# Attention and a routed expert layer on one core: three shifts in the order of the expert stage

## The chip, the cores and the metric

One Trainium2 chip, one of its cores. The metric is the device time of one execution in microseconds (us). Engine names as in the profile: PE is TensorE (PEld its weight loads), DVE is VectorE, ACT is ScalarE, POOL is GpSimd, SP is the queue that issues most DMAs.

## The reference

Block-causal attention, then a layer of eight experts in which every expert takes exactly `cap` tokens. Cut to what matters:

```python
# attention: q, k, v are (8, 8, 576, 64); causal in blocks of 64
attn = softmax(where(block_i >= block_j, q @ k.T / 8, -1e9))
x = (attn @ v).transpose(0, 2, 1, 3).reshape(4608, 512)
# experts: E = 8, cap = 4608 // 8 = 576, w1 (8, 512, 1024), w2 (8, 1024, 512)
logits = x @ w_gate
for idx in argsort(-logits.flatten()):          # the best pairs (token, expert) first
    tok, e = idx // E, idx % E
    if assigned[tok] < 0 and counts[e] < cap:
        assigned[tok] = e; counts[e] += 1
for e in range(E):
    m = assigned == e
    out[m] = maximum(x[m] @ w1[e], 0) @ w2[e]
```

## The kernel before

Two stages run one after the other: attention, up to about 343 us, and the experts. Each matrix of the expert layer is kept as a sum of two float16 parts, so a product takes three matmuls.

**Who sets the order.** The kernel's engines take their instructions in the order in which the program emits them. That order is made by a small planner (`Sched`) while the program is built. Each strand of work is a Python generator; a `yield` names an engine, an estimated cost in ns, and events that must have been set. The planner picks the strand that can start first by its own clock (`sc.now`); a lower number of priority goes ahead, and a strand of a later number may fill in where it ends early enough. `sc.set(e)` sets an event at the planned time, and `sc.ev[e]=t` sets it at a time written by hand. Such a time shapes only the written order: on the chip an instruction waits for its data, and all behind it on its engine wait with it.

**Routing.** Experts are filled one at a time, in an order that the data decide. `route(k)` searches the threshold that gives some expert `cap` tokens: 14 steps, each with counts on VectorE (L810) and ScalarE (L752), a product on TensorE (`tot`, L824) and a comparison (L827). From the result come the expert's number, with which `weights(k)` starts its loads, a prefix product (`po`, L879 to L886) that gives each token its place, and `invert`, which turns places into a list of tokens: one-hots `OH`, `OL`, `RH` on VectorE (L920, L924, L926, L927), 36 small products (`pe`, L935), a second product (`ps`, L942), and the index tile `ix` (L945). The generator `out()` (L905 to L907) takes the tokens of this expert out of the logits `Lm` and then starts `route(k+1)`, whose first instruction is L721. `route(k)` also waits until the expert `k-2` is at its middle (`mid`). The last routing has no search, since one expert is left; `hold` keeps back its two products.

**Tokens.** `gather(k)` issues five indirect DMAs on POOL (L1007), 128 rows each and 64 in the last, into `xg`. For the first two experts `flip` transposes them on TensorE (L1017), eight transposes to a block, and ScalarE and VectorE copy the halves into `X` (L1021, L1022); for the others a DMA on SP transposes them (L1032).

**Weights.** Eight pieces for each expert, loaded over SP (L993). ScalarE scales and rounds them (L972, L976), POOL subtracts to get the second part (L978); for the first four pieces of the first two experts it is L965 on ScalarE and L967 on VectorE.

**The expert.** `ffn(k)`: `h` (L1057) in two parts of the tokens, 256 and 320 wide, then `y` (L1082, and L1086 for the last 64 tokens). ScalarE and VectorE take `h` out of PSUM (L1043, L1045); ScalarE takes `y` (L1065), and POOL scatters it to the output (L1073).

Of the kernel before, what the change touches and what calls it, by code (L numbers as in the profile page):

```python
# [614 lines left out]
class Moe:  # L615
# [96 lines left out]
    def route(s,k):  # L712
# [155 lines left out]
        def full():  # L868
            V.tensor_tensor(s.es,s.es,ei,op=OP.subtract)
            V.tensor_scalar(u,oh,-8.0,None,op0=OP.mult)  # L870
            V.tensor_tensor(Lm,Lm,be(u),op=OP.add)
            sc.busy(D,520)
# [27 lines left out]
        if not last:  # L900

            def out():
                yield D,600
                if k==0: full()
                V.tensor_tensor(q[:,2],q[:,2],MM[:,0],op=OP.add)  # L905
                V.tensor_scalar(q[:,3],q[:,2],8.0,None,op0=OP.mult)
                V.tensor_tensor(Lm,Lm,b3(q[:,3]),op=OP.subtract)  # L907
                sc.set(('Lm',k+1))
                sc.add(s.route(k+1),0,sc.now)
            if k>1: sc.add(out(),0,sc.now)  # L910
            else: s.late=out
        yield from s.invert(k,L16,h2)
    def hold(s,k):

        s.sc.ev['hold',k]=s.sc.now+(8000 if k==s.E-1 else 0)
    def invert(s,k,L16,h2):
        nc=s.nc; rp=s.rp; C=s.C; V=nc.vector; sc=s.sc
        yield D,440
        OH=rp.tile([P,20,C],F16,tag="OH",name=f"OH{k}"); RH=rp.tile([P,2,20,C],F16,tag="RH",name=f"RH{k}")
        V.tensor_tensor(OH,s.io5,h2[:,None,:].to_broadcast([P,20,C]),op=OP.is_equal)  # L920
        if k<2: nc.scalar.activation(RH[:,1],OH,AF.Copy,scale=s.pc)
        yield D,700
        OL=rp.tile([P,32,C],F16,tag="OL",name=f"OL{k}",bufs=1)
        V.tensor_tensor(OL,s.iom,L16[:,None,:].to_broadcast([P,32,C]),op=OP.is_equal)  # L924
        yield D,440 if k<2 else 800
        V.tensor_tensor(RH[:,0],OH,s.tok,op=OP.mult)  # L926
        if k>1: V.tensor_scalar(RH[:,1],OH,s.pc,None,op0=OP.mult)  # L927
        else: sc.add(s.late(),0,sc.now)
        s.hold(k)
        yield T,350,'rt',('hold',k)  # L930
        tk=sc.take(); ps=s.ps.tile([P,512],F32,tag="rt",name=f"pe{k}")

        for c in range(C):
            g=32*(c%4)
            nc.tensor.matmul(ps[g:g+32,:40].rearrange("p (a b) -> p a b",a=2),lhsT=OL[:,:,c],rhs=RH[:,:,:,c],start=(c<4),stop=(c>=C-4))  # L935
        t=rp.tile([P,2,20],F16,tag="ixt",name=f"ixt{k}")
        yield D,100
        V.tensor_copy(t,ps[:,:40].rearrange("p (a b) -> p a b",a=2)); sc.set(tk)
        yield T,150,'rt'
        tk=sc.take(); ps=s.ps.tile([P,512],F32,tag="rt",name=f"ps{k}")  # L940
        for b in range(4):
            for a in range(2): nc.tensor.matmul(ps[32*b:32*b+32,0:5],lhsT=s.b32[:,a],rhs=t[:,a,b::4],start=(a==0),stop=(a==1))  # L942
        ix=rp.tile([P,5],I32,tag="ix",name=f"ix{k}",bufs=3)
        yield D,82
        V.tensor_copy(ix,ps[:,:5])  # L945
        sc.set(tk)
        sc.add(s.gather(k,ix),1,sc.now); sc.set(('ix',k))
        if k==0:

            s.wu=s.ps.tile([P,512],F32,tag="g",name="warm",bufs=4)  # L950
            for n in range(s.NWU): nc.tensor.matmul(s.wu,lhsT=s.ones,rhs=OL.rearrange("p a b -> p (a b)")[:,:512],start=True,stop=True)
            sc.free[T]=max(sc.free[T],sc.now)+213*s.NWU+1500
        s.ix[k]=ix
# [45 lines left out]
    def gather(s,k,ix):  # L999
        nc=s.nc; fp=s.fp; sc=s.sc  # L1000
        tl=[]
        for m in range(5):
            n=P if m<4 else 64
            yield G,1038,('ffn',k-2),('xm',k-1,m)
            if m==0: X=s.X[k]=fp.tile([P,8,576],F16,tag="X",name=f"X{k}")
            xg=fp.tile([P,1024],F16,tag="xg",name=f"xg{k}_{m}",bufs=5)
            nc.gpsimd.indirect_dma_start(out=xg[:n],out_offset=None,in_=s.xd,in_offset=bass.IndirectOffsetOnAxis(ap=ix[:n,m:m+1],axis=0))  # L1007
            sc.soft(728,('xg',k,m))
            sc.nolat()
            if m==4: sc.set(('gi',k))  # L1010
            sc.add(s.flip(k,m,n,xg,X),1,sc.now)
# [138 lines left out]
```

## Time and profile before

| | |
|---|---|
| median of 3 runs | 794.29 us (793.48 to 797.81) |
| profiled execution | 791.57 us |
| its span, first to last instruction | 789.8 us |
| granted TensorE clock, mean | 0.975 |
| busy share: PE, DVE, ACT, POOL | 91%, 72%, 68%, 59% |

A profile line such as `421.12 0.62 PE L1017 MATMUL xt<-m_idh,xg ... x8 [1.78 <-DMA xg<-x,ix]` gives the start, the duration, the engine, the source line, the tiles, how many instructions were merged, and, in brackets, how long the engine was idle before it and what ended that. In the list of waits the three numbers are us in total, times, and the longest. In the table of windows each engine has its busy us and, in brackets, its instructions; PEclk is the granted share of TensorE's clock. Ends of matmuls are modelled, so one that is followed at once can seem to last longer than the step from its start to the next start.

### The profile page before, as it was taken

What the parts mean: (1) busy time and instruction counts of PE and PEld (TensorE: products, weight loads), DVE (VectorE), ACT (ScalarE), POOL (GpSimd) and SP (SyncE); (2) the same over time, 40 slices, a digit from 0 to 9 for tenths busy, and PEclk for the clock granted to TensorE, in tenths of its full rate; (3) what the DMA queues carried; (4) which work ended last, traced back from release to release, by engine and by line L of the source; (5) the groups of instructions that cost most, each with busy time, mean ns of one, the idle gap of its engine ahead of it and who ended that gap; (6) DMA issues with size and microseconds to landing.
All of it is one profiled execution on the core that took longest, in us unless ns stands there. A gap on an engine that the chain in (4) does not pass through costs nothing.

```text
span 789.8 us, 19021 instructions
## 1 busy us (share of the span) xinstructions
PE 715.5 (91%) x6528; PEld 476.6 (60%) x6528; DVE 570.4 (72%) x2310; ACT 539.2 (68%) x1455; POOL 466.5 (59%) x509
## 2 busy tenths in 40 slices
PE   5779998899989999936998999999999999999995
PEld 3556776667767777724545747647466475574752
DVE  6899798998899889577988978769686793620210
ACT  5788888888988898715836868594975848283210
POOL 5788888898889876413413447373763907764001
PEclk9899999999999999966999999999999999999998
DMA  9879999999998993347026076481926639851001
GB/s 202 160 150 174 214 189 224 172 151 229 205 192 178 216 181 77 91 106 252 23 98 230 8 245 150 176 199 67 279 71 220 145 103 259 260 136 41 21 20 40
DMA packets 244305, 121.51 MB, mean 154 GB/s; under 512 B 200816, under 2 KB 227312, under 8 KB 244208
## 3 DMA queue, kind: packets, MB, share of 16 engines
q1 hardware_dynamic: 238320, 101.42, 56.7%
q0 software_dynamic: 5888, 18.88, 7.6%
q8 instruction: 51, 0.84, 0.4%
q14 instruction: 46, 0.38, 0.2%
HBM read 71.32 MB, written 18.87 MB: 114 GB/s over the span
## 4 chain that ended last, share of the span: by engine, by line
PE 42%; ACT 3%; DMA 3%; DVE 3%; issue 3%; POOL 1%; SPq 0%; POOLq 0%; another core or an unknown queue 0%; ACTq 0%; DVEq 0%
PE h L1057 23%; PE y L1082 15%; PE y L1086 2%; DMA raw<-in_moe_w_dram 1%; DMA out_dram<-yo,ix 1%; DMA xg<-x,ix 1%; POOL xg L1007 1%; ACT W L976 1%; ACT ja L752 1%; ACT raw L972 1%; DVE OL L924 1%; DVE h L897 1%; PE pe L935 1%; PE tot L824 1%; DVE jk L810 0%
## 5 line engine op out<-in xcount | busy, mean ns | idle before, releaser
L438 POOL TENSOR_TENSOR P<-P,m 128x320 f32<-128x320 f32 (+8 forms) x285 | 209.5, 770 | 49.6 <-DVE m L430 32.5
L1057 PE MATMUL h<-X,W 128*128 128x320 f16 (+3 forms) x1536 | 195.7, 286 | 0.6 <-issue 0.4
L1057 PEld LDWEIGHTS <-W 128*128 128x128 f16 x1536 | 142.0, 98 | 44.3 <-issue 4.7
L416 ACT ACTIVATE P<-psb,m 128x576 f32<-128x576 f32 (+8 forms) x288 | 149.5, 543 | 27.5 <-DVE m L409 18.7
L1082 PE MATMUL y<-W,HH 128*128 128x512 f16 x512 | 152.7, 380 | 0.0
L978 POOL TENSOR_TENSOR W<-raw,W 128x1024 f16<-128x1024 f32 x56 | 118.4, 2135 | 41.6 <-ACT W L976 36.0
L405 DVE TENSOR_REDUCE m<-psb 128x1 f32<-128x576 f32 (+8 forms) x288 | 124.8, 480 | 12.3 <-PE psb L380 11.8
L463 PE MATMUL psb<-mident,P 128*128 128x128 f32 x800 | 106.3, 281 | 13.2 <-POOL P L438 5.9
L1073 POOL DMA_INDIRECT out_dram<-yo,ix x40 | 39.3, 982 | 113.7 <-ACT yo L1065 77.5
L380 PEld LDWEIGHTS <-qT 128*64 128x64 f16 x1408 | 76.6, 111 | 43.6 <-issue 28.9
L463 PEld LDWEIGHTS psb<-mident,P 128*128 128x128 f32 x800 | 87.7, 142 | 24.5 <-POOL P L438 8.5
L380 PE MATMUL psb<-kT,qT 128*64 128x288 f16 (+8 forms) x704 | 89.6, 281 | 11.7 <-ACT P L416 10.9
L498 PE MATMUL psb<-PT,V 128*64 128x448 f32 (+5 forms) x776 | 97.2, 388 | 2.3 <-DVE PT L446 1.8
L1043 ACT ACTIVATE HH<-h 128x320 f16<-128x320 f32 (+3 forms) x128 | 52.3, 411 | 67.7 <-PE h L1057 63.3
L1082 PE MATMUL y<-W,HL 128*128 128x512 f16 x256 | 97.2, 380 | 0.0
L1007 POOL DMA_INDIRECT xg<-x,ix x40 | 40.9, 1023 | 83.0 <-DVE ix L945 38.9
L1045 DVE SCALAR_TENSOR_TENSOR HL<-h,HH 128x320 f16<-128x320 f32 (+3 forms) x128 | 56.9, 452 | 42.5 <-ACT HH L1043 39.4
L444 ACT ACTIVATE PT<-psb 128x512 f32<-128x512 f32 (+1 forms) x165 | 82.6, 593 | 4.5 <-PE psb L463 4.4
L380 PE MATMUL psb<-kS,qT 128*64 128x288 f16 (+8 forms) x704 | 82.0, 278 | 1.6 <-DVE kS L350 1.4
L1082 PEld LDWEIGHTS <-HH 128*128 128x128 f16 x512 | 47.0, 98 | 51.9 <-issue 1.3
L972 ACT ACTIVATE raw<-raw 128x512 f32<-128x512 f32 x112 | 67.7, 627 | 4.5 <-DMA raw<-in_moe_w_dram 4.5
L498 PEld LDWEIGHTS psb<-PT,V 128*64 128x64 f32 x776 | 49.5, 137 | 33.4 <-issue 24.4
(216 smaller groups left out, 1044.1 us busy)
## 6 DMA issues: line engine op xcount, KB each, us to landing
raw<-in_moe_w_dram SPq DMA_DIRECT2D x64, 512.0 KB
x<-XR SPq DMA_DIRECT2D x8, 1152.0 KB
kn<-in_k_dram SPq DMA_DIRECT2D x15, 576.0 KB
qn<-in_q_dram SPq DMA_DIRECT2D x15, 576.0 KB
V<-in_v_dram SPq DMA_DIRECT2D x64, 128.0 KB
V<-in_v_dram SPq DMA_DIRECT2D x16, 64.0 KB
xg<-x,ix POOLq DMA_INDIRECT x40
out_dram<-yo,ix POOLq DMA_INDIRECT x40
```

Source lines behind the costliest of these rows:

```text
L380: nc.tensor.matmul(out if len(K1.shape) == 2 else out.rearrange("p (r j) -> p r j", r=2), lhsT=A[:, h, 64 * i:64 * i + 64], rhs=K1, start= ...
L405: nc.vector.tensor_reduce(m[:, 0, c:c + 1], ps[:, o:o + 64 * (i + 1)] if g else s.part(ps, g, i, o), axis=AX.X if g else AX.XY, op=OP.max)
L416: nc.scalar.activation(out, in_, AF.Exp, bias=m[:, 1, c:c + 1], scale=s.ESC, accum_out=m[:, 2, c:c + 1])
L438: nc.gpsimd.tensor_tensor(sl, sl, m[:, 3, c:c + 1].to_broadcast([P, w]), op=OP.mult)
L444: s.nc.scalar.activation(out, in_, AF.Copy)
L463: nc.tensor.transpose(ps[:, a], s.Pb[n % s.NP][:, s.OFF[i] + 128 * j:s.OFF[i] + 128 * j + P], s.ident)
L498: nc.tensor.matmul(ps[64 * h:64 * h + 64, 64 * (i0 - b0):64 * (b1 - b0)], lhsT=vn[:, j, 2 * (n % 2) + h, :], rhs=pt[:, s.PTI[(j, i0)]:s.PT ...
L972: nc.scalar.activation(raw[:,x],raw[:,x],AF.Copy,scale=s.WS)
L978: nc.gpsimd.tensor_tensor(lw,raw,hi,op=OP.subtract)
L1045: nc.vector.scalar_tensor_tensor(HL[:,f,ts],ps,0.0,HH[:,f,ts],op0=OP.max,op1=OP.subtract)
L1057: nc.tensor.matmul(ps,lhsT=W[:,a,d,f*P:f*P+P],rhs=X[:,4*(d//2)+d%2+l,ts],start=(d==0 and n==0),stop=(d==3 and n==2))
L1082: if m<4: nc.tensor.matmul(ps,lhsT=Z[:,f,m*P:m*P+P],rhs=Y[:,a,f],start=(f==n==0),stop=(f==7 and n==2))
```

## The change

Three parts of the expert stage's plan change; the instructions themselves stay the same.

1. `gather`: the events `xg` of the second expert (k=1) are set 2500 ns later, so that the planner places its row transposes later.
2. `route` and `invert`: `out()` is now queued, for every routing but the last, behind the one-hots. Before, this held for the first two alone; for routings 2 to 6 it was queued as soon as the places were split (L897, L899).
3. `hold`: the last routing's two products are held back 14000 ns of planned time each, where it was 8000.

```diff
-            if k>1: sc.add(out(),0,sc.now)
-            else: s.late=out
+            s.late=out
...
     def hold(s,k):
-        s.sc.ev['hold',k]=s.sc.now+(8000 if k==s.E-1 else 0)
+        s.sc.ev['hold',k]=s.sc.now+(14000 if k==s.E-1 else 0)
...
         if k>1: V.tensor_scalar(RH[:,1],OH,s.pc,None,op0=OP.mult)
-        else: sc.add(s.late(),0,sc.now)
+        if k<s.E-1: sc.add(s.late(),0,sc.now)
         s.hold(k)
...
             sc.soft(728,('xg',k,m))
+            if k==1: sc.ev['xg',k,m]+=2500
             sc.nolat()
```

## The prediction

> **What bounds the kernel now.** I read the page first, then TensorE's waits from 350 us on, then a table of windows cut at the first matmul of each expert, then TensorE's timeline where that table shows idle time.
>
> ```profile
> PE 715.5 (91%) x6528; PEld 476.6 (60%) x6528; DVE 570.4 (72%) x2310; ACT 539.2 (68%) x1455; POOL 466.5 (59%) x509
> ...
> PE xt L1017 <- DMA xg<-x,ix: 5.4, 4, 2.7
> ...
> PE pe L935 <- DVE RH L927: 1.4, 1, 1.4
> ...
> core 0: us, PE busy (x) PEld busy (x) DVE busy (x) ACT busy (x) POOL busy (x), PEclk, DMA share, GB/s
> 419.34:430.11 10.77, 7.76 (x70) 4.27 (x71) 7.63 (x35) 5.37 (x13) 4.01 (x4) 0.84 0.61 219
> 418.47:421.88 3.41, 1.50 (x14) 0.70 (x11) 2.48 (x10) 1.72 (x4) 2.58 (x3) 1.00 1.04 388
> 421.88:425.30 3.42, 2.83 (x17) 1.65 (x18) 2.21 (x12) 2.23 (x5) 1.01 (x1) 0.50 1.03 363
> ...
> 430.11:479.94 49.83, 49.83 (x384) 30.56 (x382) 41.13 (x225) 39.07 (x96) 24.52 (x16) 1.00 0.45 140
> 479.94:531.38 51.44, 50.09 (x384) 30.89 (x383) 40.20 (x220) 38.87 (x95) 30.16 (x21) 1.00 0.62 168
> 531.38:582.24 50.86, 50.49 (x383) 30.56 (x382) 39.60 (x213) 36.77 (x90) 31.81 (x21) 1.00 0.54 153
> 582.24:633.45 51.21, 50.44 (x381) 30.66 (x382) 38.88 (x209) 35.17 (x84) 27.52 (x19) 1.00 0.55 153
> 633.45:685.18 51.73, 50.36 (x416) 31.12 (x416) 33.54 (x106) 28.10 (x61) 27.49 (x19) 1.00 0.73 212
> ```
>
> TensorE has work nearly all the time once the experts run: from 430.11 to 685.18 us it idles 0.00 + 1.35 + 0.37 + 0.77 + 1.37 = 3.9 us. A change here can only gain where TensorE stands still or runs slowly, and two such places lie on its own queue, which takes matmuls in the written order. One is 419.34 to 430.11, between the first and the second expert: 10.77 us for 7.76 of busy time, a stretch of it at a granted clock of 0.50. The other is the 1.37 us at the last routing's index product (L935).
>
> **Edit 1: the second expert's row transposes (L1017) later in the plan.** The planner now believes each gathered block `xg` lands 2.5 us later, so it writes other TensorE work ahead of the transposes.
>
> ```profile
> 418.96 0.38 PE L1082 MATMUL y<-W,HL 128*128 128x512 f16 x1
> 421.12 0.62 PE L1017 MATMUL xt<-m_idh,xg 128*128 128x128 f16 x8 [1.78 <-DMA xg<-x,ix]
> 421.57 0.17 PE L824 MATMUL tot<-cn,m_bo 128*128 128x3 f16 x1
> 422.21 1.03 PE L1017 MATMUL xt<-m_idh,xg 128*128 128x128 f16 x8 [0.47 <-issue]
> ...
> 424.79 0.85 PE L1017 MATMUL xt<-m_idh,xg 128*128 128x128 f16 x8 [0.27 <-DMA xg<-x,ix]
> ...
> 426.37 0.94 PE L1017 MATMUL xt<-m_idh,xg 128*128 128x128 f16 x16
> 427.25 0.62 PE L1086 MATMUL y<-W,HH 128*64 128x512 f16 x4
> ...
> 429.23 0.18 PE L824 MATMUL tot<-cn,m_bo 128*128 128x3 f16 x1 [0.50 <-DVE jk L810]
> ...
> 579.30 1.42 PE y L1086 x12
> ```
>
> TensorE waits 1.78 us for the first block while it still has matmuls of the first expert to do that need no transposes: three of L1082 and 24 of L1086. At full clock the whole stretch holds 3 x 0.216 = 0.65 (from starts 0.216 apart), 24 x 0.118 = 2.84 (L1086 x12), 40 transposes at 0.88 per 16 (426.37 to 427.25) = 2.2, and about 0.4 for four `tot` products with their switches: 6.1 us. So 10.77 - 6.1 = 4.6 us is the most that can go. With a shift of 2.5 us I write the queue as: L1082, three of the four groups of L1086 (0.65 + 2.13, to 422.1), blocks 0 and 1 (they landed by 421.12 and about 422.2; to 423.0), the last group and the `tot`s (to 423.9), then block 2, whose data came at 424.79: 0.9 us of waiting stays. The second expert's first half needs blocks 0 and 1 alone (L1053), so `h` starts about 425.3, with blocks 3 and 4 (0.9 us) among its matmuls. I keep 0.5 us of waiting on a late `tot`, as at 429.23. Gain: 4.6 - 0.9 - 0.5 = **3.2 us**. Bounds: 4.6 if all waits go; 0 if a later wait takes it.
>
> A longer idle stretch also lowers the clock: 1.91 us idle in 418.47:421.88 is followed by 3.42 us at 0.50, whereas the 1.37 us idle of the other place left the clock at 1.00. With 0.9 left I expect 1.00; a second half-speed stretch would take back about 1.7 us (3.42 x 0.5). [...]
>
> What else moves: event `fl` of the second expert follows its last transposes, and the loads of its second weights (SP) are written behind it. SP has nothing else to issue there, so the loads are not later on the queue, but ScalarE's and GpSimd's conversions of those four pieces are planned later (the slower rival).
>
> **Does the gain last to the end?** The next expert must be ready 3.2 us earlier.
>
> ```profile
> 449.90 2.13 POOL L978 TENSOR_TENSOR W<-raw,W 128x1024 f16<-128x1024 f32 x1 [1.17 <-ACT W L976]
> ...
> 464.68 0.98 POOL L1007 DMA_INDIRECT xg<-x,ix  x1 [2.69 <-DVE bs L691]
> ...
> 474.02 6.34 POOL L978 TENSOR_TENSOR W<-raw,W 128x1024 f16<-128x1024 f32 x3
> ...
> 479.94 0.83 PE L1057 MATMUL h<-X,W 128*128 128x256 f16 x6
> ```
>
> The third expert's fourth weight piece is finished at 474.02 + 6.34 = 480.36 and first used three groups of 0.33 behind 479.94, at 480.9: 0.5 us of spare, less than the gain. But that POOL work runs without a break behind the gathers at 464.68, which wait for the index tile, which waits for the third search. That search shares the stall: VectorE is busy 7.63 of 10.77 us in it, so it has up to 3.1 us to win back, and edit 2 brings the index tile forward by 1.4. Together 4.5 us against 3.2 - 0.5 = 2.7 needed. I take all 3.2 as kept.
>
> **Edit 2: the next logits' update (L905 to L907) behind the one-hots, for routings 2 to 6.**
>
> ```profile
> 458.74 0.19 DVE L905 TENSOR_TENSOR q<-q,MM 128x36 f32<-128x36 f32 x1
> ...
> 459.18 0.46 DVE L907 TENSOR_TENSOR m_Lm<-m_Lm,q 128x288 f32<-128x288 f32 x1
> 459.56 0.53 DVE L920 TENSOR_TENSOR OH<-m_io,h 128x720 f16<-128x720 f16 x1
> 460.00 0.45 DVE L721 TENSOR_REDUCE m_vm<-m_Lm 128x36 f32<-128x288 f32 x1
> ...
> 461.86 0.40 DVE L927 TENSOR_SCALAR RH<-OH,m_pc 128x720 f16<-128x720 f16 x1
> ...
> 551.02 0.46 DVE L907 TENSOR_TENSOR m_Lm<-m_Lm,q 128x288 f32<-128x288 f32 x1
> ...
> 556.43 0.44 DVE L721 TENSOR_REDUCE m_vm<-m_Lm 128x36 f32<-128x288 f32 x1
> ```
>
> Nothing is added or taken away; the order on VectorE changes. The update stood 0.82 us (458.74 to 459.56) ahead of the one-hots and L721 and L737 stood among them: without them the last one-hot is done some 1.4 to 1.7 us earlier, and index product, index tile and gathers with it. The next search starts later by about 1 us, since it no longer fills gaps. From routing 4 on L721 waits for the expert's middle anyway (551.48 to 556.43, 5 us of cover). TensorE waits for neither today, so I put **0**; the bounds are 0.8 either way, the length of the piece that is moved.
>
> **Edit 3: the last routing's hold, 8 to 14 us, used twice (L874, L929).**
>
> ```profile
> 668.11 6.30 POOL L978 TENSOR_TENSOR W<-raw,W 128x1024 f16<-128x1024 f32 x3
> 669.19 5.27 DVE L897 TENSOR_SCALAR h<-q 128x36 f16<-128x36 f32 x1
> 675.07 5.39 DVE L924 TENSOR_TENSOR OL<-m_iom,L 128x1152 f16<-128x1152 f16 x1
> ...
> 675.61 4.22 POOL L978 TENSOR_TENSOR W<-raw,W 128x1024 f16<-128x1024 f32 x2
> ...
> 681.27 0.92 PE L935 MATMUL pe<-RH,OL 128*32 128x40 f16 x36 [1.37 <-DVE RH L927]
> ...
> 733.29 23.63 PE h L1057 x192
> ```
>
> L897 and L924 take 5.27 and 5.39 us where other routings need 0.18 and 0.75, both while POOL subtracts weights: so the one-hots come late and TensorE stands 1.37 us. The first product moves 6 us, to about 674.7, the second 12, to about 692, inside `h` of the seventh expert. L897 would then run at 675, before POOL's next pair, OH or OL stays locked to about 680, and the last one-hot is ready near 682, ten before its product. Gain **1.37 us**; the product's own 0.92 stays. Behind it the five gathers move to about 694 to 700 and their five transposes on SP follow them; POOL's conversions of the last weights move back by some 2 us; all that is wanted at 733.29, 20 us later. Bounds: 1.4 gained, 0.8 lost if the two VectorE copies hold up `h` evictions.
>
> **Sum.** 3.2 + 0 + 1.4 = 4.6 us, on a span of 789.8 us and an execution of 791.57. The median of the runs is 794.29, 2.7 above that execution, so the forecast is 794.3 - 4.6 = 789.7.
>
> **Rivals.**
> - The gain is taken back at the third expert: the search does not win time, POOL's last piece stays at 480.36, only 0.5 us and the 1.4 remain: 792.4. For it: 0.5 us of spare; against it: VectorE's idle time in the stall.
> - A lock: the next routing's L737 and L739, now later, meet POOL's conversions, as L924 did, and the transposes behind them on TensorE's queue wait for one conversion of 2.15: 791.9. Against it: POOL mostly sits behind the gathers then. [...]
> - Slower: the second expert's last weight piece, done at 449.90 + 2.13 = 452.0, is first used 18 matmuls into `y`, about 458.4, 6.4 us of spare. Edit 1 takes 3.2 of it by the earlier TensorE and 2.5 by the later plan, leaving 0.7. It decides once ScalarE's order slips more than that; a slip of 5.3 (the two first pieces are at 438.84 and 444.18) stalls TensorE 4.6, and 1.7 more by half clock: 794.3 - 4.6 + 6.3 = 796.0.
>
> ```profile
> 438.84 2.14 POOL L978 TENSOR_TENSOR W<-raw,W 128x1024 f16<-128x1024 f32 x1 [3.55 <-ACT W L976]
> 444.18 2.14 POOL L978 TENSOR_TENSOR W<-raw,W 128x1024 f16<-128x1024 f32 x1 [3.20 <-ACT W L976]
> ```
>
> **How the numbers follow.** Forecast 0.54, third expert 0.22, lock 0.12, slower 0.12. Within 0.5% means 4.0 us here, about what a measurement can tell: 790.3 to 798.3. The forecast lies just past that line; its own range, 787.5 to 791.0, leaves 0.06 short of it, so faster 0.48; a slip over 7.5 us makes 0.07 of the slower rival cross 798.3; the rest, 0.45, is the same. The low end takes edit 1 at 4.6, edit 3 at 1.4 and half of the 2.5 us of waits in the third to fifth expert, which a new order may remove: 787.0, set at 786.5. The high end reaches to the slower rival's first half: 795.8.
>
> **What would show it.** Right: `h` of the second expert starts near 425 to 426 with a granted clock of 1.00 from 419 on; the third starts about 3 us earlier, with no wait on weights; L935's last product has no wait and lies near 690; L905 follows L927. Wrong: a new wait of TensorE at 455 to 482, or longer `tot` waits in the later searches, whose order is planned anew throughout.

## Result and profile after

The changed kernel takes 789.05 us (median of 15 runs) against 792.75 for before in the same comparison: ratio 0.9949, 95% interval 0.9930 to 0.9969. Timed again in a second comparison it gave 0.9948 (0.9918 to 0.9977). The gain of 0.5% is real and small. Medians of before differ by more than that from one comparison to the next (788.9 to 796.7), so ratios are taken inside a comparison; where two comparisons are set side by side below, the text says so.

The windows of the changed kernel, cut like those of before: first the stall, then one row from each expert's first product to the next one's.

```profile
core 0: us, PE busy (x) PEld busy (x) DVE busy (x) ACT busy (x) POOL busy (x), PEclk, DMA share, GB/s
418.89:428.44 9.55, 7.74 (x70) 3.93 (x69) 8.21 (x37) 6.00 (x13) 4.21 (x4) 1.00 0.85 311
428.44:478.64 50.20, 50.20 (x392) 30.94 (x390) 42.46 (x230) 39.16 (x97) 25.61 (x17) 1.00 0.46 140
478.64:530.10 51.46, 50.08 (x383) 30.84 (x381) 40.92 (x222) 38.99 (x95) 31.30 (x21) 1.00 0.59 162
530.10:582.02 51.92, 50.35 (x382) 30.61 (x381) 37.88 (x203) 36.30 (x87) 31.10 (x21) 1.00 0.57 156
582.02:633.13 51.11, 50.38 (x383) 30.54 (x382) 39.27 (x210) 35.26 (x85) 27.44 (x20) 1.00 0.54 153
633.13:682.39 49.26, 49.22 (x373) 30.27 (x371) 28.58 (x108) 28.47 (x61) 25.96 (x18) 1.00 0.73 212
```

The stall runs at a granted clock of 1.00 where a part of it had 0.50 (it also does in two kernels without edit 1, as a later section shows). The third expert follows without a wait (50.20 busy of 50.20). The last row is 2.5 us shorter than before's 51.73, partly because its index product now lies in the next stretch. The fourth expert's row is 1.1 us longer than before's 50.86: a wait that was not there. Inside the stall, on TensorE:

```profile
420.64 0.38 PE L1082 MATMUL y<-W,HL 128*128 128x512 f16 x1
...
422.60 0.62 PE L1017 MATMUL xt<-m_idh,xg 128*128 128x128 f16 x8
423.55 0.62 PE L1017 MATMUL xt<-m_idh,xg 128*128 128x128 f16 x8 [0.34 <-issue]
...
425.63 0.62 PE L1017 MATMUL xt<-m_idh,xg 128*128 128x128 f16 x8 [0.58 <-DMA xg<-x,ix]
427.08 0.62 PE L1017 MATMUL xt<-m_idh,xg 128*128 128x128 f16 x8 [0.83 <-DMA xg<-x,ix]
427.63 0.62 PE L1086 MATMUL y<-W,HH 128*64 128x512 f16 x4
...
428.44 0.49 PE L1057 MATMUL h<-X,W 128*128 128x256 f16 x3
428.86 0.40 PE L1017 MATMUL xt<-m_idh,xg 64*128 64x64 f16 x8
```

Blocks 0 and 1 no longer wait for data. Blocks 2 and 3 still do, 0.58 and 0.83 us, and both stand ahead of `h`; only block 4 lies inside it. The last routing (lines of this file are one lower from the changed lines on: L899 is `L16`, L934 the index product):

```profile
675.06 4.84 DVE L899 SCALAR_TENSOR_TENSOR L<-q,h 128x36 f16<-128x36 f32 x1
...
681.38 0.40 DVE L926 TENSOR_SCALAR RH<-OH,m_pc 128x720 f16<-128x720 f16 x1
...
691.68 0.93 PE L934 MATMUL pe<-RH,OL 128*32 128x40 f16 x36
```

VectorE has one long instruction (4.84 us) instead of two (5.27 and 5.39), the last one-hot is done at 681.78, and the index product comes 9.9 us later with no wait. The new wait is at 572.94, with what led to it on SP and ScalarE:

```profile
564.57 0.38 SPq L992 DMA_DIRECT2D raw<-in_moe_w_dram  x1
...
571.71 0.63 ACT L971 ACTIVATE raw<-raw 128x512 f32<-128x512 f32 x1 [2.02 <-DMA raw<-in_moe_w_dram]
572.25 0.55 ACT L752 ACTIVATE ja<-m_PB,cd 128x324 f16<-128x324 f32 x1
...
572.94 0.16 PE L824 MATMUL tot<-cn,m_bo 128*128 128x3 f16 x1 [1.48 <-ACT ja L752]
```

The last raw piece of weights, issued at 564.57 once POOL had freed its buffer, is there only at 571.7. Its scaling stands ahead of the sign count on ScalarE, the `tot` product waits for the count, and all of TensorE waits behind it. Two more `tot` products wait in this trace, 1.32 us at 519.09 and 0.68 at 612.66; no raw piece is late there, and what they wait for stands below under the late weight piece.

### The profile page after: what moved, and what is told of

It is laid out like the page before. It is cut to its first block, busy times and chain, and to the rows that moved or that the text cites. A ratio compares the mean times of both kernels' runs of the same rounds, so it can differ in the third digit from the quotient of the medians.

```text
span 787.3 us, 19016 instructions
## 1 busy us (share of the span) xinstructions
PE 719.1 (91%) x6528; PEld 479.5 (61%) x6528; DVE 564.6 (72%) x2310; ACT 539.7 (69%) x1455; POOL 466.8 (59%) x509
## 4 chain that ended last, share of the span: by engine, by line
PE 38%; issue 5%; DMA 4%; ACT 4%; POOL 2%; DVE 0%; POOLq 0%; SPq 0%; ACTq 0%; DVEq 0%
PE h L1057 20%; PE y L1082 15%; DMA raw<-in_moe_w_dram 2%; PE y L1086 2%; POOL xg L1006 2%; ACT ja L752 1%; DMA out_dram<-yo,ix 1%; ACT W L975 1%; DMA xg<-x,ix 1%; ACT raw L971 1%; POOL W L977 1%; PE pe L934 1%; PE tot L824 0%; ACT yo L1065 0%; ACT HH L1043 0%
## 5 line engine op out<-in xcount | busy, mean ns | idle before, releaser
L380 PE MATMUL psb<-kT,qT 128*64 128x288 f16 (+8 forms) x704 | 91.7, 286 | 10.9 <-ACT P L416 9.8
L380 PE MATMUL psb<-kS,qT 128*64 128x288 f16 (+8 forms) x704 | 83.8, 283 | 0.3 <-DVE kS L350 0.2
```

Source lines behind the costliest of these rows:

```text
L380: nc.tensor.matmul(out if len(K1.shape) == 2 else out.rearrange("p (r j) -> p r j", r=2), lhsT=A[:, h, 64 * i:64 * i + 64], rhs=K1, start= ...
```

## Experiments

Kernels of one comparison ran on the same chip and share its runs of before. Ratios are to before. Behind the first comparison (before, changed) there are three: A holds the edits alone and edits 1 and 3; B the changed kernel again, before and changed with 8 raw buffers, and the changed kernel with blocks split; C edits 1 and 2, the second hold alone, edit 1 with 8 buffers, and the changed kernel with 8 buffers, split. A stretch is the time from one expert's first product to the next one's, in the profiled execution; kernels whose order is the same up to there can be compared to see how it scatters.

| kernel | ratio (95%) | stretches 0 to 6, us |
|---|---|---|
| before | 1 | 60.87 49.83 51.38 50.85 51.21 51.73 48.11 |
| changed | 0.9949 (0.9930 to 0.9969) | 58.56 50.21 51.46 51.92 51.11 49.26 48.28 |
| changed, again | 0.9948 (0.9918 to 0.9977) | 58.44 50.20 49.95 50.83 51.06 49.27 48.29 |
| edit 1 alone | 1.0036 (1.0012 to 1.0060) | 58.46 50.18 49.63 51.63 54.42 54.59 47.06 |
| edit 2 alone | 1.0000 (0.9979 to 1.0020) | 60.69 49.69 49.93 49.90 50.83 51.43 47.06 |
| edit 3 alone | 1.0004 (0.9977 to 1.0031) | 60.71 49.69 50.02 50.22 53.69 49.16 48.27 |
| edits 1 and 3 | 0.9979 (0.9954 to 1.0003) | 58.96 50.18 49.65 51.97 50.79 49.17 48.28 |
| edits 1 and 2 | 0.9970 (0.9943 to 0.9996) | 58.61 50.20 51.51 51.24 52.55 52.27 47.75 |
| second hold alone | 0.9958 (0.9934 to 0.9982) | 60.91 50.18 52.23 51.83 51.19 49.16 49.19 |
| before, 8 raw buffers | 0.9969 (0.9943 to 0.9996) | 61.43 50.01 49.55 50.64 49.87 51.70 47.06 |
| edit 1, 8 raw buffers | 0.9947 (0.9924 to 0.9971) | 58.02 51.17 49.79 51.14 50.64 55.49 48.13 |
| changed, 8 raw buffers | 0.9917 (0.9889 to 0.9945) | 58.89 50.21 49.94 49.91 50.05 49.25 48.27 |
| changed, blocks split | 1.0073 (1.0047 to 1.0099) | 56.78 52.07 59.82 51.39 51.74 49.16 48.25 |
| changed, 8 buffers, split | 0.9942 (0.9919 to 0.9965) | 56.64 54.53 51.65 49.97 53.90 49.26 48.27 |

**Each edit alone, and the two without the logits' update.**

```diff
 # edit 1
-            sc.soft(728,('xg',k,m))
+            sc.soft(728,('xg',k,m)); sc.ev['xg',k,m]+=2500 if k==1 else 0
 # edit 2
-            if k>1: sc.add(out(),0,sc.now)
-            else: s.late=out
+            s.late=out
...
-        else: sc.add(s.late(),0,sc.now)
+        if k<s.E-1: sc.add(s.late(),0,sc.now)
 # edit 3
-        s.sc.ev['hold',k]=s.sc.now+(8000 if k==s.E-1 else 0)
+        s.sc.ev['hold',k]=s.sc.now+(14000 if k==s.E-1 else 0)
```

> Only the 2500 ns on the second expert's gather events. My theory (the whole gain is idle time on TensorE's own queue): the stretch between the first and second expert shrinks by 2.4 us as in the changed kernel (waits of about 0.3, 0.6 and 0.8 us left), half clock there gone, last index product still waits 1.4 us; time 2 to 2.5 us below before. Rival (the gain is taken back at the third expert, whose weights were ready only 0.5 us ahead): the second expert starts 2.4 us earlier, the third no more than 1 us earlier, total within 1 us of before.

Stretch 0 fell by 2.4 us as expected, stretches 1 and 2 kept it, and yet the kernel is 0.36% slower, which neither theory had. The gathers for the third expert began at 462.89 us, 1.8 earlier than before's 464.68 and without edit 2, so the third search did win back its share of the stall. In this profile the time went into stretches 4 and 5. TensorE's waits in the trace of edit 1 alone (sum, count, longest, in us):

```profile
PE tot L824 <- ACT ja L752: 5.7, 5, 2.2
PE pe L935 <- DVE RH L927: 2.6, 1, 2.6
```

Two windows of the same trace, at that last wait and just behind it:

```profile
681.05:684.46 3.41, 1.66 (x46) 1.03 (x50) 1.89 (x4) 0.00 (x0) 1.28 (x2) 1.00 1.03 395
684.46:687.88 3.42, 3.42 (x26) 1.53 (x26) 0.16 (x1) 0.00 (x0) 2.12 (x3) 0.50 0.55 197
```

So 5.7 us went into waits for sign counts and 2.6 into one for the last index product, and half clock (0.50) follows that one. How much of this belongs to the order and how much to one execution shows beside edits 1 and 3, below.

> Only the next logits' update behind the one-hots for routings 2 to 6. My theory: index tiles come 1.4 us earlier, next searches about 1 us later, TensorE waits for neither: within 0.8 us of before. Rival: this edit is what puts the new 1.5 us wait of a count product (tot) into the fourth expert's stage: slower by 1 to 1.5 us, and the wait near 572 us is in its trace. The old stall at 419 us is still there, with a stretch of half clock behind it if idle time of 1.8 us is what lowers the clock.

No gain or loss is shown alone. The 1.5 us wait near 572 us is not in it (stretch 3 is 49.90), so the rival falls. Its profiled execution is short, 785.0 us of span, but the 12 runs are not: one profile of this kernel says little about a quarter of a per cent.

> Only the last routing's hold at 14 us. My theory: the wait of 1.37 us before the last index product goes and nothing comes in its place: 1.4 us below before; the stretch from the sixth to the seventh expert's first product shortens by 2.3 us and the next one grows by 0.9 us. Rival: the vector engine's copies of the index product hold up evictions and take 0.8 us back: 0.5 us below before. The stall at 419 us is unchanged.

The wait is gone, and stretches 5 and 6 together are 97.43 us (99.84 before), 2.4 less. The runs show nothing of it beside an interval of 0.5%. In its profile stretch 4, whose order is that of before, is 2.5 us longer: one `tot` product waits 2.07 us, behind a late raw piece, and half clock follows (0.50 from 619.39 to 622.80).

> Both other edits without the logits' update. If the update is worth nothing (my theory) this equals the changed kernel: 3.7 us below before. If the update causes the new wait of 1.5 us in the fourth expert (rival), this is 1 to 1.5 us faster than the changed kernel: about 5 us below before. If the edits need the earlier index tile for the third expert (the prediction's step), it is slower than the changed kernel by up to 1.4 us.

0.9979, and no verdict between the theories: the interval overlaps that of the changed kernel. The wait near 573 is here too (1.49 us), without edit 2. All five six-buffer profiles with edit 1 and unsplit blocks have a late raw piece there (a `tot` product waits 0.63 to 1.49 us at 568 to 573 us), and none of the four without edit 1 has one, so it comes with edit 1.

This kernel and edit 1 alone have the same order on every engine up to the last routing, and ran in the same comparison. Yet stretch 4 is 50.79 us here and 54.42 there: these 3.6 us are scatter between two executions, and not the order's. Stretches 5 and 6, where the hold acts, are 97.45 us against 101.65, 4.2 less, and the medians of the runs differ by 5.1 (787.18 against 792.29), with intervals apart. So the hold took back what edit 1 lost alone, by the profiles for the most part at the last index product.

**The late weight piece.**

```diff
-                if n>=6: yield S,25,'hw',('wc',k,n-6)
-                elif k>0: yield S,25,'hw',('wc',k-1,n+2),('fl',1) if k==1 and n>=4 else None
+                if n>=8: yield S,25,'hw',('wc',k,n-8)
+                elif k>0: yield S,25,'hw',('wc',k-1,n+0),('fl',1) if k==1 and n>=4 else None
...
-                    raw=wp.tile([P,1024],F32,tag="raw",...,bufs=6)      # both places
+                    raw=wp.tile([P,1024],F32,tag="raw",...,bufs=8)
```

> The changed kernel once more, beside the three kernels below. If its 0.5% holds wherever it is timed, it is again 3 to 4 us below before; if its size belongs to the first comparison (each stage's waits on count products differ by 1 to 2 us from execution to execution of the same order), it is 0 to 2 us below, as the two-edit kernel was. Stage 419 to 430 must again be 2.3 to 2.4 us shorter and the last index product without a wait.

The gain held. Stretch 0 is 2.4 us shorter, the last index product does not wait, and stretches 2 and 3, with the same order as the first time, are 1.5 and 1.1 us shorter: the wait of 1.32 us at 519.09 is not there, and the one in stretch 3 is 0.63.

> The changed kernel with 8 buffers for raw weight pieces where there were 6, so that no piece waits for the vector-like subtraction on POOL of the piece six before it. Theory: the waits of TensorE for count products (1.3, 1.5 and 0.7 us in the changed kernel) come from a scaling on ScalarE that stands in front of the sign count and waits for the seventh or eighth raw piece; they go, and the time falls by 2 to 3.5 us below the changed kernel. Rival: the counts are late because the searches themselves are late (VectorE); then nothing changes, within 1 us.

From 415 to 760 us these are all of TensorE's waits:

```profile
PE xt L1017 <- DMA xg<-x,ix: 1.2, 2, 1.0
PE xt L1017 <- DVE X L1022: 0.4, 1, 0.4
```

No `tot` product waits any more in this profile. In comparisons A and B, every `tot` product of a six-buffer kernel that waited over 0.5 us behind 500 us had ScalarE idle for 0.7 to 2.4 us just ahead of its count, in front of the scaling of a raw piece (L972). In the four profiles with 8 buffers no `tot` product waits behind such an idle scaling. So the late piece is one cause. It is not the only one: of the changed kernel's three waits, it explains the 1.48 us alone. The other two follow an engine that read TensorE's result late. VectorE's comparison (L827) starts 0.24 us behind its product in the median of each profile, but at 519.09 the wait goes back to one that came 1.31 us behind its product (515.64), with VectorE idle, and at 612.66 to ScalarE's copy of the transposed logits (L747), 1.40 us behind its product where 0.31 is usual. The clearest such case is in the changed kernel with 8 buffers, split:

```profile
470.34 0.17 PE L824 MATMUL tot<-cn,m_bo 128*128 128x3 f16 x1
...
473.79 0.16 DVE L827 SCALAR_TENSOR_TENSOR sg<-tot,m_wk 128x3 f32<-128x3 f32 x1 [3.52 <-PE y L1082]
...
475.46 0.18 PE L824 MATMUL tot<-cn,m_bo 128*128 128x3 f16 x1 [3.00 <-DVE jk L810]
```

Comparisons that come 0.65 to 3.45 us late with VectorE idle stand in all six profiles of the first comparison and of C, and in none of the eight of A and B, whatever the edits and the buffers. So they go with the comparison and not with an edit; what makes them is open.

The median is 784.05 against 785.57 of the changed kernel beside it, 1.5 us less, where 2 to 3.5 were expected; the two intervals overlap. This is the fastest kernel of the study by its ratio, 0.9917.

> Before, with 8 buffers for raw weight pieces. Theory of the late piece: waits for count products in the third to fifth expert (2.3 us in the profiled execution) go, the wait at 419 us and the one at the last index product stay: 1.5 to 2.5 us below before. Rival: unchanged within 1 us.

2.2 us by the medians, 0.9969, in size as the theory has it. The waits that it named in before's profile (1.14 us at 521.53, 0.77 at 613.45) are of the other kind, though, a late reader; in this order the late piece shows in the profile of edit 3 alone (2.07). With 8 buffers on both sides the three edits are worth 787.46 - 784.05 = 3.4 us.

> Only the 2500 ns on the gather events, with 8 buffers for raw weight pieces. Theory: what the first edit alone lost (0.4% slower than before) are waits for count products behind late raw pieces, 5.7 us in its profile, and a longer wait at the last index product; with 8 buffers the first go and the second stays: 2 to 4 us below before, its fourth to fifth expert stretch back from 54.4 to about 50 us. Rival: the order of the edit is bad in itself; it stays at or above before.

Edit 1 with 8 buffers is 0.9947, in another comparison than edit 1 alone (A) and than the 0.9969 of the buffers alone (B). Stretch 4 is at 50.64 and no count waits for a raw piece, while the index product still waits 2.56 us and 6.8 us of half clock stand there. That most of edit 1's loss was the late piece does not follow: stretch 4 is as short with six buffers in edits 1 and 3 (50.79).

**Blocks 2 to 4 behind the start of `h`.**

```diff
             sc.soft(728,('xg',k,m))                 # the changed kernel
-            if k==1: sc.ev['xg',k,m]+=2500
+            sc.ev['xg',k,m]+=(2500 if m<2 else 4500) if k==1 else 0
```

> The changed kernel with blocks 0 and 1 of the second expert planned 2.5 us later as there, blocks 2 to 4 planned 4.5 us later, so that the second expert's products start before those blocks. Theory: the waits of 0.6 and 0.8 us that the changed kernel keeps there are waits for blocks 2 and 3 alone; they go and the second expert starts about 2 us earlier (its own stretch holds the transposes of blocks 2 to 4, 1.3 us, instead): a net 1 to 1.5 us. Rival: the second expert then waits for the evictions of blocks 0 and 1, and nothing is won.

Stretch 0 lost another 1.7 us, as the theory has it, but stretch 1 grew by 1.9 (the transposes of blocks 2 and 3 lie in it now, and a `tot` product waits 0.93 us at 476.96), so the third expert starts no earlier: 108.85 us for both against 108.64. And stretch 2 grew by 8 to 10: the third expert ran into its weights.

```profile
474.69 1.00 POOL L1073 DMA_INDIRECT out_dram<-yo,ix  x1 [0.17 <-issue]
482.06 0.96 POOL L1073 DMA_INDIRECT out_dram<-yo,ix  x1 [6.37 <-DMA X<-xg]
483.04 6.28 POOL L978 TENSOR_TENSOR W<-raw,W 128x1024 f16<-128x1024 f32 x3
...
485.23 1.68 PE L1057 MATMUL h<-X,W 128*128 128x256 f16 x7 [6.87 <-POOL W L978]
```

POOL's timeline and one line of TensorE's: the fourth piece's subtraction (483.04) was written behind a scatter of the output that could not start for 6.37 us. TensorE waited 6.87, and from 481.69 to 488.52 it had half clock: the seven products behind the wait start 0.21 us apart (485.23 to 486.70), where 18 of them take 1.99 us in before, 0.11 each.

> Changed kernel, 8 raw buffers, and blocks 2 to 4 planned 4.5 us later. With 6 buffers that split cost 6.9 us of TensorE at the third expert, where the fourth weight piece stood on POOL behind a scatter that waited; in this order the four pieces stand ahead of it. Theory (POOL's order was the whole loss): that wait is gone, the first stretch is 57 us as in the split kernel, and the time is 1 to 1.5 us below the changed kernel with 8 buffers. Rival: an earlier second expert always runs into the third expert's weights; a wait of 2 us or more at 478 to 486 remains.

The fourth piece stood ahead of the scatter and that wait is gone, which bears out what the split kernel's trace shows: POOL's order was the cause. It is a weak test, since the third expert itself started late here, behind the wait of 3.0 us shown above, and so needed its weights later. Two more waits for `tot` (1.4 and 2.1 us) also follow a late reader and not a raw piece. No gain over the unsplit kernel is shown.

**The hold.**

> The changed kernel with the last routing's hold back at 8 us. Theory: the last index product waits again for its one-hots, 1 to 2.6 us (1.0, 1.4 and 2.6 in the kernels with 8 us), and above some 2 us a stretch of half clock follows: 1 to 4 us slower than the changed kernel. Rival: the hold is worth nothing once the other two edits are in; equal to the changed kernel.

```diff
 # changed kernel, with before's hold
-        s.sc.ev['hold',k]=s.sc.now+(14000 if k==s.E-1 else 0)
+        s.sc.ev['hold',k]=s.sc.now+(8000 if k==s.E-1 else 0)
```

The wait is back (1.8 us), stretches 5 and 6 are 2.5 us longer. 0.9970 against 0.9949 and 0.9948 points the same way, with overlapping intervals.

> Before, with 14 us at the second use of the hold alone (ahead of the index product), 8 us at the first (ahead of the position product). Theory: only the second use matters; the wait at the last index product goes as with both, the one-hots are late as before (two vector instructions of about 5 us), and the time equals the kernel with both holds: within 0.5 us. Rival: the first use gains by moving the vector work behind POOL's subtractions; then this one keeps part of the wait.

```diff
-        s.hold(k)                          # ahead of the index product
+        s.hold(k,14000)                    # with hold(s,k,t=8000)
```

The wait is gone and stretch 5 is 49.16, as with both holds, so the second use alone takes the wait away; the one-hots are late as before (5.27 and 5.36 us). Stretch 6 is 49.19 against 48.27 with both, 0.9 longer, with a wait of 0.68 us in front of an `h` product at 700.62 that the profile gives no reason for, so that the first use is worth nothing is not shown. Its time, 0.9958, is better than that of edit 3 alone in another comparison; the intervals touch and I take no difference from it.

## Why the prediction was right

Right in sign and nearly in size: 4.6 us forecast, 3.7 measured by the two medians (4.0 by the ratio). That 789.7 came within 0.7 us of 789.05 is partly luck: the forecast started from 794.29, a median of three runs, and fifteen runs of before gave 792.75. The parts were less good than the sum: edit 1 gave less than forecast in the profiles, edit 3 more, and the two errors nearly cancel.

- **Edit 1, 3.2 us.** Measured: stretch 0 is on average 60.80 us in the four six-buffer profiles without it and 58.61 in the five with it, and stretch 1 is 0.35 longer: 1.84 net. Two terms of the step were mis-sized. The bound of 4.6 counted the half clock as lost time; edit 2 alone and the second hold alone have the same stall at full clock (1.00 in 419.60:430.00 and in 422.37:430.40), and their stretch 0 is 60.69 and 60.91 against 60.87. The matmuls go faster there (0.62 us for a block's eight transposes where before has up to 1.03) and wait longer for the same blocks, as TensorE's timeline of edit 2 alone has it (before's waits were 1.78, 0.47 and 0.27):

```profile
421.45 0.62 PE L1017 MATMUL xt<-m_idh,xg 128*128 128x128 f16 x8 [1.79 <-DMA xg<-x,ix]
...
422.64 0.62 PE L1017 MATMUL xt<-m_idh,xg 128*128 128x128 f16 x8 [0.57 <-DMA xg<-x,ix]
...
424.51 0.62 PE L1017 MATMUL xt<-m_idh,xg 128*128 128x128 f16 x8 [0.60 <-DMA xg<-x,ix]
```

  The window over that stall, in the same trace, with a granted clock of 1.00:

```profile
419.60:430.00 10.40, 7.11 (x75) 4.00 (x75) 8.09 (x36) 5.26 (x14) 4.07 (x4) 1.00 0.66 234
```

  And I placed block 3 inside `h`; it stands ahead of it and its data set the start, 0.83 us of waiting that I did not count.
- **The gain kept at the third expert.** Right for this order: no wait in stretch 1. The search won back the time, as the gathers of edit 1 alone show (1.8 us earlier); edit 2's share was not needed, since edit 1 alone kept the gain too (stretches 1 and 2). That it hung on POOL was right, as the split shows; the danger was not the 0.5 us of spare but what stands ahead of a subtraction on its queue.
- **Edit 2, 0.** Right alone, as far as the runs can tell. In its trace the last one-hot of the third routing is done 1.55 us earlier behind L899 (2.08 us against 3.63), as forecast, but the index tile only 0.6 (5.02 against 5.61): in neither trace did the index product wait for the one-hots, it came in its written place. Whether edit 2 is worth something beside edit 1 is open. Edits 1 and 2 are 0.9970 and edit 1 alone 1.0036, intervals apart, but from two comparisons; the changed kernel and edits 1 and 3, which differ in edit 2 alone, are 0.9949 and 0.9979, also from two comparisons, and their intervals overlap.
- **Edit 3, 1.4.** The wait went as described, with no price behind it, and the product lay where forecast (691.68). Pairs of profiles that differ in the hold alone show 2.4 us over stretches 5 and 6 for before, 2.5 for the changed kernel and 4.2 for edit 1. The wait is no constant: 1.4 us in before, 1.0 with edit 2, 1.8 with edits 1 and 2, 2.6 with edit 1, and again 1.4 and 2.6 for before and edit 1 with 8 buffers. It is not that TensorE reaches the product earlier: it does so 46.5 to 46.6 us into stretch 5 in all six. The one-hots come later. With edit 1 and no edit 2, the index tile of stretch 5 and the POOL work behind it stand 1.3 us later in the stretch than in before, the first long vector instruction (L897) takes 6.49 us instead of 5.27, and half clock follows the waits of 2.6 us (0.50 from 684.46 to 687.88 in edit 1 alone, 6.8 us of it with 8 buffers). Edit 1 alone, VectorE and TensorE:

```profile
669.51 6.49 DVE L897 TENSOR_SCALAR h<-q 128x36 f16<-128x36 f32 x1
...
682.80 0.92 PE L935 MATMUL pe<-RH,OL 128*32 128x40 f16 x36 [2.57 <-DVE RH L927]
```

  So edit 3 protects what edit 1 wins, and edits 1 and 3 together gain more than the two ratios alone, of the same comparison, add up to (0.9979 against 1.0036 and 1.0004).
- **"Longer `tot` waits in the later searches"** stood among what would make it wrong. They came (1.48 us at 572.94, with edit 1), cost some of the gain in the first profile, and are, with the late readers, the largest scatter here: stretches 2 to 4 sum to 153.4, 153.9 and 155.3 in three kernels of one order up to there (before, edit 3 alone, second hold alone), and to 154.5, 151.8 and 155.3 in three of the other (the changed kernel twice, edits 1 and 2).
- **Rivals.** The lock rival named L737 and L739, and neither took over 0.47 us in the changed kernel. A long vector instruction does appear where edit 3's section put one, in the last routing (L899, 675.06 to 679.90, 4.84 us where the other routings need 0.20), while POOL subtracts weights (675.63 to 679.84), but off TensorE's path. The slower rival's wait for the second expert's last piece did not appear: no wait in stretch 1.

## What to carry to other kernels

Where one queue holds all the work in a written order, a wait is taken out by writing later what is late, but look then at what the moved queue will reach earlier: here one edit alone lost 0.4% until a second one (the hold) took out the wait that it ran into. When counts or small products wait, follow the chain back through every in-order queue (product, count, scaling, load, buffer, subtraction) to the resource that is short; and look at a second profile of the same order before a wait is put down to the order, since some of these waits came and went from execution to execution. And price a stall by when its data arrive, not by its idle time plus a slow clock: here the stretch with the stall took as long with a clock of 1.00 there (60.69 us, edit 2 alone) as with 0.50 in a part of it (60.87, before).

## What the hardware showed that I had not expected

In the traces of before and of the changed kernel the granted clock changes only at times that lie whole multiples of 3.413 us apart: in before half clock lasts from 421.88 to 425.30, 3.413 us, and the full clock behind it 358.40, 105 times as long; in the changed kernel the two last stretches ahead of the final one are 27.307 and 409.599 us, 8 and 120 times. The length of a stall alone does not set the half clock: before is idle for 3.01 us of its stall (10.77 - 7.76), with 0.50 in a part of it, and edit 2 alone for 3.29 (10.40 - 7.11) at 1.00 throughout. So I look at the idle time inside one window of 3.41 us and at the clock of the next. Edit 3 alone had 2.07 us idle in one, and the next ran at 0.50:

```profile
615.97:619.39 3.42, 1.35 (x8) 0.60 (x7) 0.87 (x9) 2.26 (x6) 3.42 (x2) 1.00 0.85 249
619.39:622.80 3.41, 3.41 (x11) 1.24 (x9) 2.07 (x13) 3.23 (x9) 2.89 (x3) 0.50 0.80 142
```

Five more windows at full clock, the changed kernel's longest wait among them:

| kernel, window | TensorE idle, us | matmuls | clock of the next window |
|---|---|---|---|
| before, 418.47:421.88 | 1.91 | 14 | 0.50 |
| edit 1 alone, 681.05:684.46 | 1.75 | 46 | 0.50 |
| edits 1 and 2, 610.37:613.78 | 1.98 | 7 | 1.00 |
| changed, 569.90:573.31 | 1.48 | 11 | 1.00 |
| before, 677.88:681.29 | 1.37 | 14 | 1.00 |

Idle time alone does not part them: 1.75 and 1.91 us were followed by half clock, 1.98 was not. The first two windows have transposes or small index products in them, the third only seven matmuls in 1.43 us of work; that this is the reason is not shown. And none of the windows behind which the clock dropped here was idle throughout: they have 1.35 to 1.66 us of work.
